# A hand-planned attention and MoE kernel: how a step chooses between two engines, and a second copy of keys made from PSUM

## The chip, the core and the metric

The kernel runs on one core of a Trainium2 chip. The metric is the device time of one execution in microseconds, the median over several runs. The core's engines are TensorE (PE, with its weight loads as PEld), VectorE (DVE), ScalarE (ACT), GpSimd (POOL) and SyncE (SP), which here only issues DMAs.

## The reference

Three layers follow each other on 4 batches of 576 tokens and 512 channels, all in fp32:

```python
# 1. windowed attention, 8 heads of 64: window 32, or 128 with every 4th key for the last 4 heads
scores = where(mask, (q @ k.T) / 8, -1e9); x = softmax(scores) @ v
# 2. mixture of 4 causal attention experts of width 64, the 2 best by x @ w_gate
for e in range(4):
    q, k, v = x @ wq[e], x @ wk[e], x @ wv[e]
    ye = softmax(where(causal, (q @ k.T) / 8, -1e9)) @ v @ wo[e]
    out += gate_weight[e] * ye
# 3. layer norm and MLP 512 -> 2048 -> 512 with a residual
return x + relu(norm(x) @ w_ch1) @ w_ch2
```

## The kernel before

Products that need more than one rounded pass are split: a value is kept as a rounded high part and a low part that holds the rest (h and l in the names), and three matmuls stand for one product.

The work is cut into small generators ("chains"): `turned_qk` and `window` (layer 1, per batch and head pair), `value_tile`, `gate`, `project` and `attend` (layer 2), `out_proj`, then `norm`, `norm_tile`, `decode` and `mlp_group` (layer 3). Each yields its steps one by one, with the engine, a duration in ns that the author assigned, and the times at which its inputs are due. The planner `run_chains` (lines 206 to 250) runs when the program is built: in a loop it looks at the next step of every chain, finds the earliest time at which it could begin on its engine, and issues the step with the lowest score; a tie goes to the chain's rank. The order in which steps are issued is the order of each engine's queue on the chip, and every queue is in order. The times in the planner are only its own; the chip runs each instruction as soon as its queue and its inputs allow.

Most steps name one engine. Steps made with `either` (line 170) name two, and the planner takes the better score: the copies out of PSUM between ACT and DVE (lines 404, 407, 479, 537, 540, 767, 785, 864), the normalisation of a window's scores (line 468) and of an expert's probabilities (line 757) between DVE and POOL, and the shift ahead of the norm's transposes (line 1022) between ACT and DVE. A star at an engine's name says that the step shares an SBUF port with the other of DVE and POOL; in the plan such a step starts only when the other engine's last starred step has ended, 80 ns later. The two choices with POOL are:

```python
t, e = yield either(("DVE*", 370.0), ("POOL*", 620.0), deps=[t])                                # 467
tpp[ee], e = yield either(("DVE*", 70.0 + 0.95 * (n - 64)), ("POOL*", 3.2 * (n - 64)), deps=[t])  # 756
```

where n is 192, 320, 448 or 576 keys for the tiles that have such a step.

`project(b, pr_)` (line 608) computes queries and keys of two experts for one batch, in two halves of 288 tokens each (`hf`); keys come first. Twelve matmuls fill a PSUM bank `pp` whose partitions 0 to 63 belong to one expert and 64 to 127 to the other (line 636). For keys, per expert `ee`: ACT rounds the expert's 64 partitions into `KH` (line 655), a DMA from SP copies these into the other 64 partitions of `KH` (line 657; the planner counts 480 ns of SP and 2200 ns until it lands), and DVE writes what rounding left out into `KL` (line 660, the KL subtract; the tile is called klz in the trace). For queries, ACT rounds into one half of `SQ` (line 648) and DVE writes the rest into the other half (line 650). In `attend` one matmul with 128 rows of `SQ` against both halves of `KH` (line 708) thus gives two of the products, and one against `KL` (line 709) the third. There are 4 batches, 2 expert pairs and 2 halves, so 16 K banks and 32 such casts, transfers and subtracts. The 8 PSUM banks are shared by all chains; `give_bank` gives one back at a planned time.

Of the kernel before, what the change touches and what calls it, by code (L numbers as in the profile page):

```python
# [9 lines left out]
I32 = mybir.dt.int32  # L10
# [13 lines left out]
def windowed_attention_moe_mlp(  # L24
# [15 lines left out]
    nc = tc.nc  # L40
# [10 lines left out]
    HS = S // 2  # L51
# [20 lines left out]
    def bank(name):  # L72

        x = taken.pop(0)
        b = ps1.tile([P, 512], F32, tag=f"bank{x}", name=name)
        lent_banks[id(b)] = x, b
        return b
# [24 lines left out]
    def late(name, dtype):  # L102

        return const.tile([P, 2 * S], dtype, tag="late", name=name, bufs=2)
# [62 lines left out]
    def op(engine, ns, deps=(), tile=None):  # L167
        return "op", ((engine, ns),), deps, tile

    def either(*engines, deps=()):  # L170
        return "op", engines, deps, None

    def acq(tag, n=1):
        return "acq", tag, n

    def key(*k):
        return "key", k
# [4 lines left out]
    def give_bank(b, at):  # L182
        places["bank"].append((at, lent_banks.pop(id(b))[0]))

    def put(*k, at):
        facts[k] = at
# [13 lines left out]
    def resume(c, value):  # L200
        try:
            c[2] = c[1].send(value)
        except StopIteration:
            chains.remove(c)

    def run_chains():
        while chains:
            again = True
            while again:
                again = False  # L210
                for c in sorted(chains, key=lambda c: c[0]):
                    kind = c[2][0]
                    if kind == "acq" and len(places[c[2][1]]) >= c[2][2]:
                        tag, n = c[2][1:]
                        places[tag].sort()
                        at = places[tag][n - 1]
                        if tag == "bank":
                            taken.extend(x for _, x in places[tag][:n])
                            at = at[0]
                        del places[tag][:n]  # L220
                        resume(c, at)
                        again = True
                        break
                    if kind == "key" and c[2][1] in facts:
                        resume(c, facts[c[2][1]])
                        again = True
                        break
            best = None
            for c in chains:
                if c[2][0] != "op":  # L230
                    continue
                _, engines, deps, tile = c[2]
                for name, ns in engines:
                    engine = name.rstrip("*")
                    at = max([free[engine]] + [d + lag[engine] for d in deps])
                    if name != engine:
                        at = max(at, shared["POOL" if engine == "DVE" else "DVE"])
                    change = MODE if engine == "PE" and tile != mode[0] else 0.0
                    score = (at + change + (ns if len(engines) > 1 else 0.0) * 0.5, c[0])
                    if best is None or score < best[0]:  # L240
                        best = score, c, name, ns, at + change, tile
            assert best is not None, [(c[0], c[2]) for c in chains]
            _, c, name, ns, at, tile = best
            engine = name.rstrip("*")
            if name != engine:
                shared[engine] = at + ns + 80.0
            free[engine] = at + ns
            if engine == "PE":
                mode[0] = tile
            resume(c, (at + ns + tail[engine], engine) if len(c[2][1]) > 1 else at + ns + tail[engine])  # L250

    def copy_by(engine, dst, src):
        (nc.scalar.copy if engine == "ACT" else nc.vector.tensor_copy)(dst, src)  # L253
# [54 lines left out]
    def last(k, n):  # L308

        left[k] = left.get(k, n) - 1  # L310
        return left[k] == 0
# [247 lines left out]
    def done_x(b, t):  # L559
        if last(("xh", b), NT + 8):  # L560
            give("xh", t)
# [46 lines left out]
    def project(b, pr_):  # L608
        tx = 0.0
        for c in range(KC):  # L610
            tx = max(tx, (yield key("x", b, c)))
        tw = max((yield key("w", 1)), (yield key("w", 2)))
        tk = (yield key("fr", b - 1, pr_)) if b else 0.0
        tq = yield acq("qk2", 4)
        xh, xl = XH[b], XL[b]

        SQ = [att.tile([P, S], F32R, tag="qk2", name="SQ", bufs=QB) for _ in range(2)]
        KH = [att.tile([P, S], F32R, tag="qk2", name="KH", bufs=QB) for _ in range(2)]
        if b == 0:

            KLZ[pr_] = late(f"klz{pr_}", F32R).rearrange("p (e s) -> p e s", e=2)
            for ee in range(2):
                yield op("POOL", 550.0, [tx])
                nc.gpsimd.memset(KLZ[pr_][64 - 64 * ee:128 - 64 * ee, ee].bitcast(F32), 0.0)
        KL = [KLZ[pr_][:, ee] for ee in range(2)]
        QK[b, pr_] = SQ, KH, KL
        for hf in range(2):
            for wh, wl, isq in ((wkh, wkl, False), (wqh, wql, True)):
                tb = yield acq("bank")
                pp = bank("pp")  # L630
                n = 0
                cs = slice(hf * HS, (hf + 1) * HS)
                for c in range(KC):
                    t = yield op("PE", 400.0, [tb, tx, tw])
                    for ws, xs in ((wh, xh), (wh, xl), (wl, xh)):
                        nc.tensor.matmul(pp[:, :HS], ws[:, c, pr_ * P:(pr_ + 1) * P], xs[:, c, cs],  # L636
                                         start=n == 0, stop=n == 3 * KC - 1)
                        n += 1
                done_x(b, t)
                if b == B - 1 and last("wqk", 8):  # L640
                    put("wqk", at=t)
                ends, dups = [], []
                for ee in range(2):
                    own = slice(64 * ee, 64 * ee + 64)
                    oth = slice(64 - 64 * ee, 128 - 64 * ee)
                    if isq:
                        a = yield op("ACT", 392.0, [t, tq])
                        nc.scalar.mul(SQ[ee][own, cs], pp[own, :HS], SCALE)
                        a = yield op("DVE", 375.0, [a])
                        nc.vector.scalar_tensor_tensor(SQ[ee][oth, cs], pp[own, :HS], SCALE,  # L650
                                                       SQ[ee][own, cs].bitcast(F32),
                                                       op0=ALU.mult, op1=ALU.subtract)
                    else:
                        a = yield op("ACT", 392.0, [t, tq])
                        nc.scalar.copy(KH[ee][own, cs], pp[own, :HS])
                        a2 = yield op("SP", 480.0, [a])
                        nc.sync.dma_start(KH[ee][oth, cs].bitcast(I32), KH[ee][own, cs].bitcast(I32))
                        a2 += 2200.0
                        a = yield op("DVE", 375.0, [a, tk])
                        nc.vector.tensor_tensor(KL[ee][own, cs], pp[own, :HS], KH[ee][own, cs].bitcast(F32),  # L660
                                                op=ALU.subtract)
                        dups.append(a2)
                    ends.append(a)
                give_bank(pp, max(ends))
                put("q", b, pr_, hf, isq, at=max(ends + dups))


    places.update(yh=[0.0], yhs=[0.0], pTh=[0.0] * 2, pT2=[0.0] * 3)
# [453 lines left out]
    with tc.manual_schedule():  # L1122
# [34 lines left out]
        for f in range(NF):  # L1157
            need = min(n for n, (fs, gi) in enumerate(jobs) if f in fs)
            for x in range(2):
                chain(41.0 + f + 0.5 * x if f < 3 else 44.0 + need - 3.0 + 0.5 * x, decode(f, x))  # L1160
        run_chains()


# [26 lines left out]
```

## Time and profile before

| | before |
|---|---|
| median of 3 runs | 770.72 us (770.51 to 774.78) |
| profiled execution | 770.02 us, of which the profile's span is 768.2 us |
| mean granted TensorE clock | 0.982 |
| busy: PE, PEld, DVE, ACT, POOL | 726.0, 603.8, 529.5, 297.0, 192.0 us |
| chain that ended last, by engine | PE 70%, DVE 20%, ACT 4% |

Times in the profile are counted from the span's start. A busy PE isn't PE at its peak, since its matmuls overlap and their ends are modelled. "x <- y" in a list of waits says that x stood idle until y ended; "issue" is a wait for nothing that the profile shows. Names of tiles come without their buffer numbers; s is a bank of scores, pp a bank of projected keys or queries, sc a window's scores, Pp an expert's probabilities, and ppt a bank of transposed ones.

### The profile page before, as it was taken

The page shows a single profiled execution, that of the slowest core. Times are in us where ns is not written, and L with a number is a line of the kernel's source. Part 1 is how long each engine was busy: PE and PEld are TensorE (multiplying, and loading weights), DVE is VectorE, ACT ScalarE, POOL GpSimd, SP SyncE. Part 2 cuts the span into 40 slices and gives each one's busy share as a digit, 9 for nine tenths or more (in the row PEclk, how much of TensorE's full clock was granted, in tenths as well). Part 3 has the DMA queues.
Part 4 walks back from the last instruction along what each step waited for, and adds up shares of the span by engine and source line. Part 5 has one row for each costly group of instructions (what it writes and reads, how often), then busy time and mean ns, then how long its engine had stood idle before and what let it go on. Part 6 is the DMA issues. An engine that isn't in the chain of part 4 may idle for free.

```text
span 768.2 us, 13813 instructions
## 1 busy us (share of the span) xinstructions
PE 726.0 (94%) x5196; PEld 603.8 (79%) x5196; DVE 529.5 (69%) x1342; ACT 297.0 (39%) x793; POOL 192.0 (25%) x233
## 2 busy tenths in 40 slices
PE   6889899999999899799997999999999999999997
PEld 5678778978887789577875888888888888888886
DVE  4756998699778888897467887476474664754333
ACT  3554766466456665774235222122121120211110
POOL 3143231033212213562003434033051140320000
PEclk8979999999999999999999999999999999999999
DMA  8582243223311222210001212011020020100123
GB/s 149 117 166 55 45 93 62 48 59 81 78 32 43 44 64 72 63 56 1 1 0 55 83 56 82 1 56 55 1 83 27 28 83 0 56 1 0 42 82 123
DMA packets 89777, 43.10 MB, mean 56 GB/s; under 512 B 74864, under 2 KB 85104, under 8 KB 89712
## 3 DMA queue, kind: packets, MB, share of 16 engines
q1 hardware_dynamic: 89712, 42.23, 22.2%
q8 instruction: 41, 0.67, 0.4%
q14 instruction: 24, 0.20, 0.1%
HBM read 35.14 MB, written 4.72 MB: 52 GB/s over the span
## 4 chain that ended last, share of the span: by engine, by line
PE 70%; DVE 20%; ACT 4%; issue 2%; SPq 2%; DMA 1%; POOL 1%; DVEq 0%; POOLq 0%; ACTq 0%
PE pout L1102 25%; PE phid L1080 25%; PE pp L636 3%; PE pv L533 3%; PE pwo L853 2%; DVE nm L722 2%; DVE sm L464 2%; DVE mx L457 1%; DVE sc L459 1%; DVE SQ L650 1%; PE po L488 1%; PE ptr L392 1%; PE s L447 1%; PE ppt L475 1%; PE ppt L781 1%
## 5 line engine op out<-in xcount | busy, mean ns | idle before, releaser
L1102 PE MATMUL pout<-wp,ht 128*128 128x512 f32 x864 | 219.7, 395 | 1.5 <-DVE ht L1087 1.3
L1080 PE MATMUL phid<-xn,wp 128*128 128x512 f32 (+1 forms) x960 | 220.0, 373 | 0.5 <-ACT xn L1040 0.5
L1080 PEld LDWEIGHTS phid<-xn,wp 128*128 128x128 f32 x960 | 169.0, 189 | 35.4 <-ACT xn L1040 0.7
L1102 PEld LDWEIGHTS pout<-wp,ht 128*128 128x128 f32 x864 | 160.1, 188 | 37.4 <-DVE ht L1087 2.5
L1111 DVE SCALAR_TENSOR_TENSOR x2a<-pout,rstd,x2a 128x512 f32<-128x512 f32 x124 | 92.2, 748 | 60.9 <-PE pout L1102 59.9
L1085 ACT ACTIVATE ht<-phid 128x512 fp32r<-128x512 f32 (+1 forms) x80 | 44.4, 555 | 203.0 <-PE phid L1080 203.0
L1087 DVE SCALAR_TENSOR_TENSOR ht<-phid,ht 128x512 fp32r<-128x512 f32 (+1 forms) x80 | 50.8, 636 | 65.7 <-ACT ht L1085 65.3
L955 POOL TENSOR_TENSOR d_pw<-d_pw,d_t 128x512 f32<-128x512 f32 x32 | 41.3, 1291 | 180.1 <-DVE d_pw L952 145.0
L468 POOL TENSOR_TENSOR sc<-sc,rs 128x288 f32<-128x288 f32 x35 | 23.3, 672 | 136.0 <-DVE rs L466 117.3
L967 POOL TENSOR_TENSOR wp<-d_pw,wp 128x512 fp32r<-128x512 f32 x32 | 44.4, 1389 | 36.4 <-ACT wp L965 36.4
L757 POOL TENSOR_SCALAR Pp<-Pp,rs 128x512 f32<-128x512 f32 (+3 forms) x34 | 39.3, 1163 | 52.6 <-DVE rs L750 39.8
L939 ACT ACTIVATE d_sq<-ws 128x512 f32<-128x512 f32 x32 | 21.6, 674 | 48.3 <-DVE d_pw L958 23.7
L965 ACT CAST wp<-d_pw 128x512 fp32r<-128x512 f32 x32 | 19.8, 619 | 47.2 <-DVE d_pw L958 41.3
L708 PE MATMUL s<-KH,SQ 128*128 128x64 f32 (+4 forms) x96 | 34.1, 364 | 4.1 <-issue 1.4
L253 ACT COPY pT<-ppt 96x384 f32<-96x384 f32 (+4 forms) x74 | 33.5, 462 | 11.1 <-PE ppt L781 6.3
L724 ACT ACTIVATE Pp<-s,nm 128x192 f32<-128x192 f32 (+3 forms) x64 | 30.4, 475 | 11.7 <-DVE nm L722 8.7
L447 PE MATMUL s<-kT,qT 64*64 64x96 f32 x576 | 34.3, 260 | 0.2 <-ACT kT L253 0.2
L392 PE MATMUL ptr<-ident,nat 72*128 72x72 f32 (+1 forms) x196 | 25.6, 254 | 9.0 <-DMA nat<-in_q_dram 8.2
L475 PE MATMUL ppt<-ident,sc 128*96 128x128 f32 x144 | 26.6, 300 | 7.0 <-POOL sc L468 2.9
L447 PEld LDWEIGHTS s<-kT,qT 64*64 64x64 f32 x576 | 31.9, 147 | 0.6 <-issue 0.5
L781 PE MATMUL ppt<-ident,Pp 128*128 128x128 f32 x160 | 28.8, 282 | 2.8 <-DVE rs L748 1.1
L709 PE MATMUL s<-klz,SQ 128*128 128x64 f32 (+4 forms) x96 | 30.8, 321 | 0.0
(162 smaller groups left out, 1339.8 us busy)
## 6 DMA issues: line engine op xcount, KB each, us to landing
ws<-in_moe_w_ch_dram SPq DMA_DIRECT2D x32, 512.0 KB
nat<-in_q_dram SPq DMA_DIRECT2D x14, 288.0 KB
nat<-in_k_dram SPq DMA_DIRECT2D x14, 288.0 KB
vt<-in_v_dram SPq DMA_DIRECT2D x16, 192.0 KB
out_dram<-x2a SPq DMA_DIRECT2D x12, 256.0 KB
KH<-KH SPq DMA_DIRECT2D x32, 72.0 KB
vt<-in_v_dram SPq DMA_DIRECT2D x32, 48.0 KB
out_dram<-x2b SPq DMA_DIRECT2D x4, 256.0 KB
```

The lines of the kernel that those rows point to most:

```text
L447: nc.tensor.matmul(ps[z, 96 * tt:96 * (tt + 1)], qT[z, 64 * t_:64 * t_ + 64], kT[z, 64 * t_:64 * t_ + 96], start=False, stop=tt == TU - 1)
L475: nc.tensor.transpose(pt[:96, P * tt:P * (tt + 1)], sc[:, tt], ident)
L708: nc.tensor.matmul(ps[:m, :z - a], SQ[ee][:, q0:q0 + m], KH[ee][:, a:z], start=True, stop=False)
L757: (nc.vector if e == "DVE" else nc.gpsimd).tensor_scalar(Ps[ee][:m, 64:n], Ps[ee][:m, 64:n], rs[:m, ee:ee + 1], None, op0=ALU.mult)
L781: nc.tensor.transpose(pt[:, P * (j - 1):P * j], Ps[ee][:, k0:k0 + P], ident)
L955: nc.gpsimd.tensor_tensor(pf, pf, t1.bitcast(F32), op=ALU.add)
L967: nc.gpsimd.tensor_tensor(lo, pf, hi.bitcast(F32), op=ALU.subtract)
L1080: nc.tensor.matmul(ph[:, :n_tok], ws[:, c * P:(c + 1) * P], xs[c], start=n == 0, stop=n == 3 * KC - 1)
L1085: nc.scalar.activation(hh[:, :n_tok], ph[:, :n_tok], AF.Relu)
L1087: nc.vector.scalar_tensor_tensor(hl[:, :n_tok], ph[:, :n_tok], 0.0, hh[:, :n_tok].bitcast(F32), op0=ALU.max, op1=ALU.subtract)
L1102: nc.tensor.matmul(po, a_[:, sl], w_, start=n == 0, stop=n == 3 * len(fs) - 1)
L1111: nc.vector.scalar_tensor_tensor(x2(i), po, rstd[:, i:i + 1], x2(i), op0=ALU.mult, op1=ALU.add)
```

## The change

Two edits. In the planner, the score of a step that may go to either of two engines no longer has half of its duration in it; the time at which it can begin counts alone, as for steps with one engine. In `project`, the second copy of the rounded keys isn't a DMA from SP any more: ACT or DVE, as the planner chooses, copies the expert's partitions of `pp` a second time, into the other 64 partitions of `KH`. This step is issued between the cast and the KL subtract, and the bank goes back when the subtract and the copy have ended.

```diff
@@ run_chains
                     change = MODE if engine == "PE" and tile != mode[0] else 0.0
-                    score = (at + change + (ns if len(engines) > 1 else 0.0) * 0.5, c[0])
+                    score = (at + change + 0.0, c[0])
                     if best is None or score < best[0]:
@@ project
-                ends, dups = [], []
+                ends = []
...
                         a = yield op("ACT", 392.0, [t, tq])
                         nc.scalar.copy(KH[ee][own, cs], pp[own, :HS])
-                        a2 = yield op("SP", 480.0, [a])
-                        nc.sync.dma_start(KH[ee][oth, cs].bitcast(I32), KH[ee][own, cs].bitcast(I32))
-                        a2 += 2200.0
+                        a2, e = yield either(("ACT", 392.0), ("DVE", 380.0), deps=[t, tq])
+                        copy_by(e, KH[ee][oth, cs], pp[own, :HS])
                         a = yield op("DVE", 375.0, [a, tk])
                         nc.vector.tensor_tensor(KL[ee][own, cs], pp[own, :HS], KH[ee][own, cs].bitcast(F32),
                                                 op=ALU.subtract)
-                        dups.append(a2)
+                        a = max(a, a2)
                     ends.append(a)
                 give_bank(pp, max(ends))
-                put("q", b, pr_, hf, isq, at=max(ends + dups))
+                put("q", b, pr_, hf, isq, at=max(ends))
```

## Rows read from the trace of the kernel before

**Rows 1.** Busy us by stage: length, PE, PEld, DVE, ACT, POOL, clock, DMA.

```profile
60.00:80.00 20.00, 18.98 (x188) 17.86 (x187) 13.00 (x45) 10.18 (x31) 3.61 (x4) 1.00 0.23 48
80.00:130.00 50.00, 46.54 (x564) 37.54 (x563) 46.28 (x171) 34.46 (x113) 12.65 (x22) 1.00 0.33 68
130.00:150.00 20.00, 19.50 (x206) 18.41 (x205) 12.17 (x43) 7.46 (x22) 0.72 (x2) 1.00 0.28 63
150.00:200.00 50.00, 47.39 (x537) 39.56 (x535) 46.59 (x167) 33.04 (x113) 17.76 (x25) 1.00 0.28 60
200.00:230.00 30.00, 28.44 (x280) 26.25 (x279) 19.77 (x65) 12.87 (x37) 4.55 (x7) 1.00 0.30 60
230.00:280.00 50.00, 46.01 (x544) 37.70 (x541) 44.32 (x153) 33.07 (x106) 10.61 (x17) 0.97 0.21 48
280.00:300.00 20.00, 19.38 (x157) 18.57 (x151) 15.42 (x42) 10.80 (x29) 5.02 (x4) 1.00 0.28 86
300.00:350.00 50.00, 43.54 (x289) 34.63 (x288) 46.45 (x134) 34.15 (x96) 28.39 (x23) 0.97 0.16 49
400.00:412.00 12.00, 7.45 (x34) 4.64 (x32) 10.12 (x22) 7.83 (x18) 4.04 (x4) 0.94 0.15 45
412.00:768.00 356.00, 351.86 (x1614) 289.17 (x1613) 210.51 (x330) 69.83 (x126) 80.92 (x63) 1.00 0.15 48
```

**Rows 2.** TensorE's waits, whole run: total us, times, longest us.

```profile
PE ppt L475 <- POOL sc L468: 2.9, 6, 1.0
...
PE s L708 <- issue: 1.4, 2, 0.8
...
PE pp L636 <- DVE klz L660: 0.7, 2, 0.6
```

**Rows 3.** TensorE's waits from 0 to 60 us, same columns.

```profile
PE ptr L392 <- DMA nat<-in_q_dram: 8.2, 2, 5.0
```

**Rows 4.** Tile KH: ns min/median/max, first and last start us.

```profile
L655 ACT CAST KH<-pp x32: 377/394/397, 61.6 to 311.6; 64x288 fp32r<-64x288 f32 x32
L657 SPq DMA_DIRECT2D KH<-KH x32: 461/494/1350, 62.0 to 312.0; - x32
```

**Rows 5.** Waits of SP's DMA queue, whole run, same columns.

```profile
SPq L657 <- ACT KH L655: 49.1, 17, 13.6
```

**Rows 6.** Groups by line: count | busy us, mean ns | idle before, releasers.

```profile
L757 POOL TENSOR_SCALAR Pp<-Pp,rs 128x512 f32<-128x512 f32 (+3 forms) x34 | 39.3, 1163 | 52.6 <-DVE rs L750 39.8 <-ACT pT L253 6.6 <-DVE n L731 2.3
...
L757 DVE TENSOR_SCALAR Pp<-Pp,rs 128x128 f32<-128x128 f32 (+3 forms) x30 | 13.0, 455 | 0.0
...
L746 DVE TENSOR_SCALAR sm<-sm 128x2 f32<-128x2 f32 x40 | 8.7, 221 | 1.0 <-ACT Pp L724 0.7
...
L253 DVE COPY kT<-ptr 128x288 f32<-128x288 f32 x16 | 7.3, 456 | 3.8 <-PE ptr L392 3.6
...
L468 DVE TENSOR_TENSOR sc<-sc,rs 128x288 f32<-128x288 f32 x13 | 5.9, 475 | 0.1
```

**Rows 7.** Waits of all engines, columns as in Rows 2.

```profile
ACT KH L655 <- DVE klz L660: 10.0, 12, 1.3
```

**Rows 8.** Chain that ended last, KL subtracts, first and last: start, us.

```profile
68.16 0.46 DVE klz L660
...
303.79 0.47 DVE klz L660
```

**Rows 9.** Busy time by stage, line 655 alone, columns as in Rows 1.

```profile
150.00:200.00 50.00, 0.79 (x2) 1.00 0.28 60
...
300.00:350.00 50.00, 1.55 (x4) 0.97 0.16 49
```

**Rows 10.** Timeline from 334 to 340 us: start us, us, engine, line.

```profile
334.30 0.15 DVE L748 RECIPROCAL rs<-sm 128x2 f32<-128x2 f32 x1
...
335.39 1.04 POOL L963 TENSOR_TENSOR d_pw<-d_pw,g_in 128x512 f32<-128x512 f32 x1 [1.85 <-DVE d_pw L958]
...
335.43 1.03 DVE L746 TENSOR_SCALAR sm<-sm 128x2 f32<-128x2 f32 x1
```


## Prediction

> **What bounds the kernel now.** Read the busy time by stage first [rows 1]. From 412 us to the end, in the second MLP, TensorE works 351.86 of 356 us at a granted clock of 1.00, its 2.4 GHz level. The change adds no instruction there, and of the steps with a choice between engines only a few ahead of the norm's transposes are left, so what it can move lies before 412 us, and it reaches the end by shifting that block. Before it two sorts of stage alternate. In the four projection stages (60 to 80, 130 to 150, 200 to 230, 280 to 300 us) TensorE idles 1.02, 0.50, 1.56 and 0.62 us, 3.7 us of 90, and VectorE is busy 60.4 of 90 us. In the four attention stages (80 to 130, 150 to 200, 230 to 280, 300 to 350 us) VectorE works 44.3 to 46.6 of 50 us, and TensorE idles 3.46, 2.61, 3.99 and 6.46 us, 16.5 us together. There VectorE is as near the bound as TensorE. One more hole stands at 400 to 412 us, 4.55 us, where the last tiles of the attention pass through the norm.
>
> Then read who ended TensorE's waits [rows 2]: behind the first loads (8.2 us in two waits, both before 60 us [rows 3]) they are single waits of 0.3 to 1 us. No one wait explains the 20 us of holes; they are many small misses of an order written out ahead.
>
> **The change part by part, against the profiled execution's 770.0 us (0.7 under the median of the runs, 770.72).**
>
> *The transfer that goes.* 32 DMA issues of 0.494 us leave SP, 15.8 us of its queue [rows 4]. SP waited 49.1 us with such an issue at its head, for the cast that feeds it [rows 5], and loads stood behind it. But TensorE's two waits for loads come before the first such issue, at 62.0 us [rows 3, 4], so I put loads that start earlier at nothing: loading ahead covers them, and without that cover a wait like the 5.0 us one would be the price. What a score matmul waited for the second half of KH is shown nowhere by name: the trace has no landing time for this transfer. The nearest row is the score matmul's own wait with no releaser the profile shows, 1.4 us in two waits [rows 2]. So the gain lies between 0 and 1.4 us, and I take half: **-0.7 us**. In the planner's count the scores also come due about 2.3 us earlier (480 + 2200 ns of transfer against a copy of 380 to 392 ns). This makes work available sooner, but in the projection stages TensorE has other work, as 3.7 us of idle in 90 say.
>
> *The copy that comes.* 32 copies of 64x288 from PSUM. On ScalarE the nearest row is the first copy of the same data, 0.394 us [rows 4]; on VectorE a copy of the same length took 0.456 us [rows 6]; so 0.43 us in the mean and 13.8 us of engine time in all. They don't run beside the work they join. The trace shows ScalarE's second cast waiting 10.0 us in 12 waits for VectorE's subtract of the first half [rows 7], though the two touch different halves of the bank: readers of a bank take turns. Each K bank is therefore held by five or six turns where there were four, 0.86 us longer. The chain that ended last passes through 18 of the 32 subtracts, from 68.16 to 303.79 us [rows 8]. If each of these is pushed by a copy, the cost is 18 x 0.43 = 7.7 us; if TensorE's other work hides all of them it is 0. I choose from two places. TensorE waited twice for a K bank's subtract [rows 2]; 0.86 us more on each is 1.7 us. And 8 of the 32 casts lie in the attention stages, from two in the stage at 150 us to four in that at 300 us [rows 9], where VectorE has no room. ScalarE has 33 to 34 of 50 us there [rows 1], and the rule below takes the engine that is free first, so I charge half of 8 x 0.43, 1.7 us. Together **+3.4 us**; what hides the rest is TensorE's own projection matmuls.
>
> The Trainium skill, page "PSUM — Partial Sum Buffer", section "PSUM bank collisions raise a hardware error", asks that two engines be kept apart per bank and group of 32 partitions, and allows different groups of one bank at once. By that finer form a copy of one half could run beside the other half's subtract, and only 16 of the 32 copies would lengthen a bank's turn: the sum would be 1.7 us lower. The trace bears out the coarser form, a whole bank at a time, and the sum goes by that.
>
> *The choice between two engines.* Before, a step that could go to either engine was ranked by its start plus half its duration. So it stood behind every fixed step that could start within that half, and the slower engine was charged half the difference. Now the start alone counts. Between ScalarE and VectorE durations are close, and little moves. Between VectorE and GpSimd it matters: for line 757 the planner's halves differ by 109 to 541 ns, for line 468 by 125 ns. On VectorE stand 30 steps of line 757 (13.0 us busy) and 13 of line 468 (5.9 us) [rows 6]. I estimate that a third of both moves, 14 steps, which takes 6.3 us off VectorE. Nothing before shows how many would move: the bounds are 0 and all of them, 18.9 us. A stage can't give back more than TensorE's holes in it, 16.5 us in all; with TensorE busy over 90% there, I count half of the relief: **-3.2 us**.
>
> Against it stand two costs. A step of line 757 takes 1163 ns on GpSimd and 455 on VectorE [rows 6], so its data comes some 0.7 us later. TensorE's waits for GpSimd were 2.9 us [rows 2] for the 35 steps of line 468 that ran there (48 windows less the 13 on VectorE), 0.083 us each; 14 more at that price are **+1.2 us** (bounds 0, and 14 x 0.7 = 9.9 us if all are waited for). And GpSimd stops VectorE: at 335.43 us a step on 128x2 values took 1.03 us while a GpSimd step of 1.04 us ran, where a step of that size took 0.15 us just before [rows 10]. The mean of that line is 221 ns [rows 6], so over 40 of them about 40 x 0.07 = 2.8 us was lost beside 34 steps of line 757 on GpSimd; ten more cost **+0.8 us** (bounds 0, and 10 x 0.9 = 9 us if each meets such a step). Page "SBUF — State Buffer" of the Trainium skill, section "Who interferes with whom", says that the second of two such instructions fully blocks until the first ends; the row agrees, and this speaks against the change.
>
> The sum: 770.0 - 0.7 + 3.4 - 3.2 + 1.2 + 0.8 = **771.5 us**. Beyond it, every later step may land in another place. One such miss is worth at most what the largest hole costs today, 4.55 us, in either direction; from this comes the forecast's own range, 766 to 777.
>
> **The rivals.** *VectorE is relieved for good (faster).* If the copies go mostly to ScalarE and two thirds of the steps leave VectorE, the holes of the four attention stages close by 60%: 16.5 x 0.6 = 9.9 us, 760 us. For it: VectorE at 93% in these stages. Against it: TensorE is itself at 92 to 95% in three of them.
>
> *The K banks' turns become the bound (slower).* Each copy stands between a cast and a subtract, and a copy on VectorE waits at the head of its queue for the cast, with the reductions and subtracts of other tiles behind it. This decides once 20 copies shift the chain (20 x 0.43 = 8.6 us); with 25 of 32 it is 770.0 + 10.8 = 781 us. For it: 18 subtracts on the chain. Against it: 0.7 us of waits for these banks now.
>
> *GpSimd's long steps come on the path (slower).* The two halves of a tile both go to GpSimd, since VectorE's turn is counted from GpSimd's end. If 13 of them are waited for in full, 13 x 0.7 = 9 us, 779 us. For it: the 1.03 us row. Against it: 0.083 us a step now.
>
> *The change doesn't do what it says.* The score matmuls did not wait for the transfer, the copies hide, and hardly a step moves: 770 us.
>
> **How the numbers follow.** About 1%, from 763.0 to 778.4 us, can't be told from no change. The forecast 0.52 (0.03 of it beyond each bound), no effect 0.08, VectorE relieved 0.17 (0.15 below 763.0), K banks 0.14 (0.11 above 778.4), GpSimd 0.09 (0.05 above). So faster 0.18, slower 0.19, within 1% 0.63. Under 760 us I leave out 0.09 (half of the faster case), over 782 us 0.09 (part of both slower cases): the range is 760 to 782.
>
> **What would show it.** Right: TensorE's idle in the projection stages stays near 4 us, the nameless waits of the score matmul are gone, line 757 on GpSimd rises from 34 to some 44, VectorE's busy time in the attention stages falls though 32 copies were added. Wrong: TensorE's waits for a K subtract rise above 3 us (banks), waits for lines 757 or 468 on GpSimd above 6 us (GpSimd), idle in the attention stages under 8 us (relief), or the hole at 400 us shut or doubled, which no term here counts. Most exposed is the third of the steps that I let move: it is an estimate from the planner's lines, not a row.

## The result and the profile after

The changed kernel takes 761.91 us (median of 4 runs, 759.07 to 762.34), the kernel before in the same comparison 770.62 us (770.04 to 774.78). The medians differ by 8.7 us, or 1.1%; the ratio, which goes by all runs, is 0.9868, with an interval from 0.9826 to 0.991, so 1.3% faster. The profiled execution took 761.55 us, of which 759.8 us are its span. In the listings of after, and of every kernel below that has after's `project`, the line numbers from 657 on are one lower: line 757 of before is L756, the KL subtract of line 660 is L659.

The busy time of the engines over the span, from the page of after:

```profile
PE 722.1 (95%) x5196; PEld 603.9 (79%) x5196; DVE 542.4 (71%) x1397; ACT 293.6 (39%) x792; POOL 163.2 (21%) x211
```

VectorE is busy 12.9 us more than before (529.5), GpSimd 28.8 us less (192.0). TensorE's idle time, span less busy, went from 42.2 to 37.7 us, its busy time from 726.0 to 722.1: 4.5 and 3.9 us, the 8.4 us between the two spans.

The busy time by stage of after, the stages and columns of [rows 1] (length, PE, PEld, DVE, ACT, POOL, clock, DMA share, GB/s):

```profile
60.00:80.00 20.00, 19.08 (x202) 18.09 (x200) 11.75 (x38) 9.40 (x28) 7.90 (x12) 1.00 0.18 33
80.00:130.00 50.00, 45.01 (x533) 38.83 (x534) 47.28 (x171) 33.97 (x115) 11.54 (x23) 1.00 0.38 80
130.00:150.00 20.00, 17.91 (x187) 15.48 (x186) 12.76 (x43) 8.44 (x25) 0.10 (x1) 1.00 0.03 5
150.00:200.00 50.00, 47.33 (x547) 41.27 (x547) 46.20 (x158) 31.51 (x107) 8.11 (x18) 1.00 0.33 71
200.00:230.00 30.00, 30.00 (x316) 26.90 (x315) 24.65 (x90) 16.29 (x48) 2.93 (x6) 1.00 0.13 29
230.00:280.00 50.00, 47.51 (x539) 41.36 (x538) 44.84 (x159) 33.52 (x105) 7.97 (x13) 1.00 0.20 48
280.00:300.00 20.00, 17.96 (x149) 15.14 (x148) 19.12 (x61) 13.22 (x37) 3.37 (x3) 1.00 0.09 27
300.00:350.00 50.00, 46.30 (x339) 37.69 (x339) 47.99 (x155) 35.10 (x99) 14.32 (x11) 1.00 0.13 43
400.00:412.00 12.00, 12.00 (x58) 9.94 (x57) 6.75 (x10) 2.17 (x4) 0.00 (x0) 1.00 0.01 1
```

Three things are to be seen against [rows 1], whose stretches are kept here. After's own stages lie a little elsewhere (its first K matmul starts at 65.4 us, that of before at 59.7), so sums of stretches say more than a single one. The hole at 400 to 412 us (4.55 us) is gone. TensorE's idle in the four attention stages fell from 16.5 to 13.85 us, that in the four projection stages rose from 3.7 to 5.05. And the granted clock, which was 0.97 at 230 to 280 and at 300 to 350 us and 0.94 at 400 to 412 us, is 1.00 in all of them. In before it fell behind idle time of TensorE, here from 310 us on:

```profile
310.00:315.00 5.00, 2.11 (x16) 1.91 (x15) 4.46 (x15) 4.10 (x12) 4.24 (x3) 0.99 0.13 30
315.00:318.30 3.30, 3.30 (x18) 2.46 (x17) 2.11 (x9) 1.33 (x4) 2.04 (x3) 0.50 0.02 5
```

Of the first 5 us TensorE was busy 2.11; in the next 3.3 us it was busy throughout, at half the clock, the 1.2 GHz level. So this hole was paid for twice, once as idle time and once in clock.

The first MLP matmul of line 1080 starts at 302.1 us where it started at 323.1, the last transpose of line 1031 at 388.4 us where it was 416.0. These marks overstate the lead: the number of matmuls is the same, and what runs earlier here is missing later. From that transpose to the end of the span after takes 371.4 us, before 352.2, and 8.4 us of the 27.6 reach the end of the span (8.7 by the medians of the runs).

TensorE's waits in after (us in total, times, longest us), those that answer [rows 2]; then VectorE's wait for ScalarE's cast, which is new, and the groups by line that answer [rows 6]:

```profile
PE ppt L475 <- POOL sc L468: 4.5, 5, 2.3
...
PE ppt L780 <- DVE klz L659: 1.7, 1, 1.7
PE pp L636 <- DVE klz L659: 1.6, 2, 1.4
```

```profile
DVE KH L253 <- ACT KH L655: 8.5, 11, 2.0
```

```profile
L756 DVE TENSOR_SCALAR Pp<-Pp,rs 128x256 f32<-128x256 f32 (+3 forms) x58 | 22.0, 418 | 0.0
...
L253 DVE CAST KH<-pp 64x288 fp32r<-64x288 f32 x18 | 8.2, 455 | 8.7 <-ACT KH L655 8.5
...
L756 POOL TENSOR_SCALAR Pp<-Pp,rs 128x128 f32<-128x128 f32 (+2 forms) x6 | 6.7, 1124 | 24.6 <-DVE rs L749 17.7 <-ACT V L549 6.9
...
L253 ACT CAST KH<-pp 64x288 fp32r<-64x288 f32 x14 | 5.5, 394 | 0.2
...
L468 DVE TENSOR_TENSOR sc<-sc,rs 128x288 f32<-128x288 f32 x7 | 3.7, 534 | 0.1
```

Of the 64 steps of line 757, 58 run on VectorE (30 before) and 6 on GpSimd (34 before): the opposite of what was forecast. Line 468 went the other way, 13 to 7 on VectorE. The copies split 18 to VectorE and 14 to ScalarE, 13.7 us of engine time, and those on VectorE stood 8.5 us at the head of its queue until ScalarE's cast of the same bank had ended.

### The profile page after: what moved, and what is told of

Read it like the earlier page. It is cut to its first block, busy times and chain, and to the rows that moved or that the text cites. A ratio compares the mean times of both kernels' runs of the same rounds, so it can differ in the third digit from the quotient of the medians.

```text
span 759.8 us, 13731 instructions
## 1 busy us (share of the span) xinstructions
PE 722.1 (95%) x5196; PEld 603.9 (79%) x5196; DVE 542.4 (71%) x1397; ACT 293.6 (39%) x792; POOL 163.2 (21%) x211
## 4 chain that ended last, share of the span: by engine, by line
PE 78%; DVE 16%; ACT 2%; issue 1%; DMA 1%; SPq 1%; POOL 0%; DVEq 0%; POOLq 0%; ACTq 0%
PE pout L1101 26%; PE phid L1079 26%; PE pp L636 4%; PE s L447 3%; PE pwo L852 3%; PE ppt L780 2%; PE ppt L475 2%; PE pv L533 2%; PE ptr L392 2%; PE po L488 2%; PE py L801 1%; PE s L707 1%; DVE Pp L756 1%; DVE xl L509 1%; DVE klz L659 1%
## 5 line engine op out<-in xcount | busy, mean ns | idle before, releaser
L954 POOL TENSOR_TENSOR d_pw<-d_pw,d_t 128x512 f32<-128x512 f32 x32 | 41.5, 1296 | 217.0 <-DVE d_pw L951 186.9
L468 POOL TENSOR_TENSOR sc<-sc,rs 128x288 f32<-128x288 f32 x41 | 27.2, 668 | 144.2 <-DVE rs L466 135.1
L253 ACT COPY pT<-ppt 96x384 f32<-96x384 f32 (+4 forms) x66 | 30.3, 466 | 20.5 <-PE ppt L475 13.3
L723 ACT ACTIVATE Pp<-s,nm 128x320 f32<-128x320 f32 (+3 forms) x64 | 30.4, 476 | 12.6 <-DVE nm L721 11.4
L707 PE MATMUL s<-KH,SQ 128*128 128x64 f32 (+4 forms) x96 | 32.5, 346 | 2.2 <-ACT pTh L253 0.9
L780 PE MATMUL ppt<-ident,Pp 128*128 128x128 f32 x160 | 28.8, 282 | 4.0 <-DVE klz L659 1.7
L462 ACT ACTIVATE sc<-sc 128x288 f32<-128x288 f32 x48 | 21.0, 445 | 26.0 <-DVE sc L459 25.8
L1110 DVE SCALAR_TENSOR_TENSOR x2b<-pout,rstd,x2b 128x512 f32<-128x512 f32 x32 | 24.0, 749 | 9.3 <-PE pout L1101 9.1
## 6 DMA issues: line engine op xcount, KB each, us to landing
vt<-in_v_dram SPq DMA_DIRECT2D x16, 192.0 KB, 3.6
```

The lines of the kernel that those rows point to most:

```text
L707: nc.tensor.matmul(ps[:m, :z - a], SQ[ee][:, q0:q0 + m], KH[ee][:, a:z], start=True, stop=False)
L780: nc.tensor.transpose(pt[:, P * (j - 1):P * j], Ps[ee][:, k0:k0 + P], ident)
L954: nc.gpsimd.tensor_tensor(pf, pf, t1.bitcast(F32), op=ALU.add)
L1110: nc.vector.scalar_tensor_tensor(x2(i), po, rstd[:, i:i + 1], x2(i), op0=ALU.mult, op1=ALU.add)
```

## The experiments

The theory at the start: the gain comes from the 28 steps of line 757 that left GpSimd for VectorE, and the copies cost little. Its rivals: the gain is the order in which steps are issued, whichever engine they go to; and the result is an accident of one order. Each kernel below is timed against the kernel before, whose median in the five comparisons was 770.24 to 771.71 us. "Rule" stands for the new choice between two engines, "order" for the whole sequence of issues that the planner writes.

### The two edits alone

The rule alone has, of the change, only the score; the transfer stays as in before. The copy alone has after's `project` with the old score.

```diff
-  score = (at + change + (ns if len(engines) > 1 else 0.0) * 0.5, c[0])
+  score = (at + change + 0.0, c[0])            # rule alone: this, in before
```

> The rule of choice alone, with the transfer from SP left as before; in its program 49 of the 64 steps of line 757 stand on VectorE (30 before, 58 after the change). Theory A (the gain of 8.7 us comes from line 757 going to VectorE, which takes 0.42 us there against 1.16 us on GpSimd): 762 to 765 us. Theory B (the gain comes from the transfer that is gone): 770 to 772 us. Theory C (it is only another order, and any order differs by some us): anything from 760 to 778 us, with no relation to the count of line 757.

> The copy alone, with half of the duration still in the score; in its program 25 steps of line 757 stand on VectorE and 39 on GpSimd. Theory A: 770 to 774 us (the copies cost engine time, and nothing else is won). Theory B: 761 to 764 us. Theory C: anything from 760 to 778 us.

Measured: rule alone 755.1 us, ratio 0.9774 [0.9747, 0.9802], 49 of line 757's steps on VectorE. Copy alone 776.3 us, 1.0049 [1.0027, 1.007], 25 on VectorE. The two edits pull in opposite directions, and the change is the smaller for its copies: the rule gives 16.6 us against this comparison's 771.71, the copy costs 4.6.

### How much one order differs from another

Each kernel issues its steps in one order, so a difference of two kernels holds the luck of two orders. To size that, a constant of the planner was moved by 2 ns, which leaves the instructions the same but for the engine of some two-engine steps and reorders them.

```diff
-    MODE = 141.0
+    MODE = 139.0                               # second order
```

```diff
-    tail = {... "DVE": 95.0, "POOL": 70.0 ...}
+    tail = {... "DVE": 97.0, "POOL": 70.0 ...}  # third order
```

> The kernel before with one of the planner's constants, the price of changing the matmul tiling, at 139 in place of 141 ns: no instruction is another, but nearly all queues are in another order (line 757: 31 on VectorE, 33 on GpSimd). Theories A and B: within 3 us of before, 768 to 774 us. Theory C: off by 5 us or more.

> The changed kernel with the same constant at 139 ns: another order, and 56 steps of line 757 on VectorE. Theories A and B: within 3 us of the changed kernel, 759 to 765 us. Theory C: off by 5 us or more, so that it may come out at 768 us as well.

> The kernel before with the planner's tail of a VectorE step at 97 in place of 95 ns: the same instructions in another order (27 steps of line 757 on VectorE). Theory C, which the first four runs favour (two reorderings moved by +6 and +15 us): 765 to 785 us, 5 us or more off in most such orders. Theory A: 768 to 775 us.

> The changed kernel with the tail of a VectorE step at 97 ns: another order, 57 steps of line 757 on VectorE. Theory C: between 755 and 780 us. Theory A: 759 to 766 us, and under the kernel before whatever the order.

> The new rule of choice with the transfer from SP, and the tail of a VectorE step at 97 in place of 95 ns: a second order of that kind (53 steps of line 757 on VectorE). Theory D, formed from the first eight runs: the rule is worth some 15 to 20 us whatever the order, and the copies cost 13 us of it again. Then 748 to 762 us. Theory C (the order alone): anything from 755 to 780 us.

> The new rule of choice with the transfer from SP, and the price of changing the tiling at 139 ns: a third order of that kind, with only 39 steps of line 757 on VectorE. Theory D: 748 to 764 us. Theory C: anything from 755 to 780 us. If it is line 757's engine that counts, this one is the slowest of the three by 3 us or more.

> The copies with the old rule of choice, and the planner's tail of a VectorE step at 97 in place of 95 ns: a second order of that kind (the first took 776.3 us; three orders of the old rule with the transfer took 770.6 to 777.6 us). If the copies cost under the old rule what they cost under the new one (10 us over three orders each, 13.4 us in one and the same order): 778 to 790 us. If the old rule hides them: 770 to 777 us.

Measured, in us (interval of the ratio in brackets; the first column is the order of the change itself):

| | as it is | MODE 139 | DVE tail 97 | mean |
|---|---|---|---|---|
| old rule, transfer (before) | 770.6 | 777.58 [1.003, 1.0097] | 773.15 [0.9996, 1.0044] | 773.8 |
| old rule, copies | 776.3 [1.0027, 1.007] | not run | 784.93 [1.0152, 1.0202] | 780.6 (of two) |
| new rule, transfer | 755.1 [0.9747, 0.9802] | 755.64 [0.976, 0.9858] | 758.6 [0.98, 0.9883] | 756.4 |
| new rule, copies (after) | 761.9 [0.9826, 0.991] | 776.64 [1.0041, 1.0085] | 761.58 [0.9807, 0.9908] | 766.7 |

The rule is no accident: with the transfer kept, all three orders of it lie 12 us or more below all three orders of the old rule, 17.4 us in the mean; with the copies it is 13.9 us by the means, and 18.9 over the two orders that both rows have. The copies cost 10.3 us under the new rule in the mean of three orders (6.8, 21.0 and 3.0), and 8.7 under the old one in the mean of two (5.7 and 11.8); the means of the table differ by 6.8 there, because one of them holds an order that was not run with copies. What is partly an accident is the size for the whole change: before against after is 8.7, 0.9 and 11.6 us in the three orders. At 0.9 us, with MODE 139, nothing of the rule's gain is left beside the copies.

The number of line 757's steps on VectorE doesn't go with the time: 49, 39 and 53 in the three orders of the rule with the transfer, which lie within 3.5 us, and 56 in the MODE 139 order of after, 14.7 us slower than after with 58. That speaks against the theory.

### The engine of line 757 by itself

```diff
-  tpp[ee], e = yield either(("DVE*", 70.0 + 0.95 * (n - 64)), ("POOL*", 3.2 * (n - 64)), deps=[t])
+  tpp[ee], e = (yield op("DVE*", 70.0 + 0.95 * (n - 64), [t])), "DVE"       # in before: all on VectorE
```

```diff
+  e = ("DVE", "POOL")[ee]                                                   # in after: half and half
+  tpp[ee] = yield op(("DVE*", "POOL*")[ee], (70.0 + 0.95 * (n - 64), 3.2 * (n - 64))[ee], [t])
```

> The kernel before with all 64 steps of line 757 given to VectorE; the old score and the transfer stay. If the rule's gain comes from keeping this line off GpSimd: 755 to 764 us. If it comes from when a step with a choice gets its turn: 768 to 776 us.

> The changed kernel with line 757 split by hand, the first half of a tile on VectorE and the second on GpSimd (32 and 32, as the kernel before has 30 and 34); the new score and the copies stay. If the rule's gain comes from keeping this line off GpSimd: 770 to 780 us. If not: 758 to 768 us.

Measured: with the old rule and all 64 on VectorE 780.87 us, 1.0124 [1.0073, 1.0174], slower than before. With the new rule and 32 on GpSimd 765.34 us, 0.9911 [0.9877, 0.9946], 3.4 us slower than after and still faster than before. The theory falls: moving the steps to VectorE by hand doesn't bring the gain, and moving 26 of them back doesn't undo it. Each of the two is one order, and the interval of the second overlaps that of after; but neither went where the theory puts it (755 to 764 us and 770 to 780 us).

### The engine or the turn

The one score of before does two things. It picks the engine of a step, and it ranks the step against the next steps of all other chains, its turn. These two kernels, with the transfer kept, take the new score for one and the old one for the other.

```diff
+  late = at + change + (ns if len(engines) > 1 else 0.0) * 0.5
+  picks.append((late, at + change, name, ns))
   ...
+  late, at, name, ns = min(picks, key=lambda x: x[0])   # turn only: engine by the old score,
+  score = (at, c[0])                                    #            turn by the start
   ...
+  late, at, name, ns = min(picks, key=lambda x: x[1])   # engine only: engine by the start,
+  score = (late, c[0])                                  #              turn by the old score
```

> The kernel before with the rule of choice taken apart: which engine a step takes still goes by its start plus half its duration, but its turn among all steps goes by its start alone. The transfer stays. If the gain of the rule (17.5 us over three orders each) lies in the turn: 753 to 762 us. If it lies in the choice of the engine: 768 to 778 us.

> The other part: the engine goes by the earliest start alone, the turn by start plus half the duration as before. The transfer stays. If the gain lies in the turn: 768 to 778 us. If it lies in the choice of the engine: 753 to 762 us.

> The turn alone by the earliest start, and the planner's tail of a VectorE step at 97 in place of 95 ns: a second order of that kind, so that the order's own spread is seen. Turn: 753 to 764 us. Engine: 768 to 778 us.

> The engine alone by the earliest start, and the tail of a VectorE step at 97 ns: a second order of that kind. Turn: 768 to 780 us. Engine: 753 to 764 us.

Measured (second value: the same with the DVE tail at 97): turn only 761.2 us, 0.9874 [0.9841, 0.9907], and 755.3, 0.9814 [0.9791, 0.9837]; engine only 766.68, 0.9959 [0.9938, 0.9979], and 776.22, 1.0077 [1.0058, 1.0097]. In the mean the turn alone gives 758.3 us, where both halves together gave 756.9 in the same two orders; the engine alone gives 771.5, where the old rule gave 771.9. Order by order the turn alone gives 9.4 and 17.9 us, the engine alone 3.9 us and then 3.1 us of loss. So the gain is that of the turn. All steps with a choice got the new turn at once, the copies out of PSUM too; which of them bring the gain was not separated. The turn also explains the count: engine only has 25 and 15 steps of line 757 on VectorE (30 and 27 by the old rule), which is the direction that the prediction forecast; turn only has 55 and 53.

What the turn does is seen ahead of the second MLP. The stretches from 60 to 280 us and from 280 to 420 us (columns as above) of before, then of turn only, turn only with tail 97, engine only, and engine only with tail 97:

```profile
60.00:280.00 220.00, 206.86 (x2302) 177.33 (x2301) 182.13 (x640) 131.08 (x418) 49.90 (x76) 0.99 0.27 58
280.00:420.00 140.00, 128.04 (x804) 104.22 (x799) 103.96 (x264) 72.22 (x187) 44.19 (x35) 0.98 0.12 38
```

```profile
60.00:280.00 220.00, 211.20 (x2295) 184.95 (x2294) 191.94 (x670) 123.74 (x405) 27.70 (x57) 0.97 0.30 60
280.00:420.00 140.00, 132.20 (x846) 106.69 (x844) 118.48 (x315) 65.86 (x177) 32.16 (x24) 1.00 0.12 38
```

```profile
60.00:280.00 220.00, 211.58 (x2356) 185.10 (x2356) 193.58 (x687) 130.63 (x424) 32.96 (x63) 1.00 0.30 64
280.00:420.00 140.00, 133.02 (x814) 105.80 (x813) 115.35 (x285) 64.66 (x169) 33.47 (x26) 1.00 0.10 34
```

```profile
60.00:280.00 220.00, 205.84 (x2288) 178.80 (x2287) 175.62 (x621) 132.97 (x429) 55.25 (x80) 0.98 0.27 59
280.00:420.00 140.00, 129.53 (x813) 105.03 (x812) 104.96 (x262) 72.84 (x190) 44.27 (x35) 0.95 0.11 34
```

```profile
60.00:280.00 220.00, 204.77 (x2285) 178.18 (x2285) 174.45 (x617) 131.97 (x430) 66.41 (x93) 0.99 0.26 57
280.00:420.00 140.00, 125.32 (x788) 102.70 (x787) 100.96 (x252) 68.35 (x181) 46.72 (x38) 0.94 0.13 39
```

From 60 to 280 us VectorE is busy 9.8 and 11.5 us more with the new turn than in before. Of this 5.9 and 4.4 us are steps of lines 757 and 468, which now stand on VectorE; 3.9 and 7.1 us are other work. TensorE is busy 4.3 and 4.7 us more. In the first order that is no more work, for it ran 2295 matmuls where before ran 2302, at a granted clock of 0.97 against 0.99; in the second it ran 54 more. With the new engine choice alone both are busy less than in before, VectorE mostly because fewer steps of these two lines stand on it. The kernel with the old rule and line 757 all on VectorE did not fill it: VectorE is busy 178.28 us there, 18.2 of them with line 757 (10.9 in before). After itself has TensorE at 206.84 us there, as its projections begin 5.7 us later than before's; its lead shows from 280 to 420 us, 133.63 against 128.04.

Over both stretches the two turns part clearly, among the kernels that keep the transfer. With the new turn (the rule alone in three orders, the turn alone in two) TensorE idles 13.1 to 17.5 us from 60 to 420 us and runs 3139 to 3194 matmuls there, at a clock of 0.98 to 1.00. With the old turn (before in three orders, the engine alone in two, line 757 all on VectorE) it idles 24.6 to 31.6 us and runs 3057 to 3100, at 0.97 to 0.99. The least and the most idle kernel of the new turn (the rule alone, and with tail 97), then of the old (engine only, and line 757 all on VectorE):

```profile
60.00:420.00 360.00, 346.94 (x3194) 295.07 (x3193) 307.25 (x959) 197.07 (x598) 88.15 (x108) 1.00 0.24 54
```

```profile
60.00:420.00 360.00, 342.53 (x3187) 292.19 (x3186) 302.94 (x958) 197.34 (x603) 75.03 (x98) 1.00 0.23 52
```

```profile
60.00:420.00 360.00, 335.37 (x3099) 283.83 (x3098) 280.57 (x882) 205.81 (x619) 99.52 (x115) 0.97 0.21 49
```

```profile
60.00:420.00 360.00, 328.39 (x3057) 278.37 (x3055) 285.29 (x913) 200.20 (x604) 51.58 (x76) 0.97 0.21 49
```

In the mean of each group the idle time differs by 12.7 us and the time of the kernel by 17.0; what makes up the rest, the clock for one, was not separated.

This agrees with one reading of the code: a step whose turn carries half its duration is issued behind fixed steps that start later than it could, and since queues are in order, what stands behind it in its chain is late as well. That TensorE's holes shrink with the turn is shown; that it is by this mechanism and no other is argued from the code.

### What the copies cost in one and the same order

This kernel lets the planner count after's copy and issues the DMA of before in its place, with the planned times unchanged; TensorE's and GpSimd's queues are the same as after's. The next issues each copy twice, under the plan of one. The last puts all 32 copies on ScalarE, under the same plan.

```diff
   a2, e = yield either(("ACT", 392.0), ("DVE", 380.0), deps=[t, tq])
-  copy_by(e, KH[ee][oth, cs], pp[own, :HS])
+  nc.sync.dma_start(KH[ee][oth, cs].bitcast(I32), KH[ee][own, cs].bitcast(I32))   # transfer
+  copy_by(e, ...); copy_by(e, ...)                                                # twice
+  copy_by("ACT", KH[ee][oth, cs], pp[own, :HS])                                   # on ScalarE
```

> The changed kernel with the planner untouched (it still counts a copy, on ScalarE or VectorE), but in place of each of the 32 copies the transfer from SP is issued. TensorE's and GpSimd's queues are the same, instruction by instruction; VectorE and ScalarE lack the copies. If the transfer's latency was what the scores waited for (theory B): slower than the changed kernel by 2 us or more, 764 to 772 us, with new waits of the score matmul. If the copy is worth nothing or costs (the sum's +3.4 us against -0.7): equal or faster, 756 to 762 us.

> The changed kernel with each of the 32 copies made twice in a row, the planner untouched: 13.8 us more of engine time, in the same order. If a copy costs what the sum counted (3.4 us for 32): 764 to 767 us. If copies lie beside TensorE's other work: 761 to 763 us. If the K banks' turns bound the stage (18 or more of them on the chain): 769 us or more.

> The changed kernel, the planner untouched, but all 32 copies run on ScalarE (18 of them stood on VectorE): VectorE is rid of 8.2 us of copies and of 8.5 us in which its queue waited at a copy for ScalarE's cast. If the 13.4 us that the copies cost are VectorE's queue: 750 to 756 us. If they are the longer turns at a K bank, whichever engine copies: 759 to 764 us.

Measured: transfer 748.5 us, 0.97 [0.9666, 0.9734]; copies 761.9; copies on ScalarE 756.33, 0.9814 [0.9783, 0.9845]; each copy twice 777.05, 1.0055 [1.0033, 1.0076]. So the copies cost 13.4 us over a transfer in the same order, and a second set of them 15.1, each for 13.7 us of engine time. A part of the second price is clock: from 60 to 331 us it was 0.97 with each copy twice and 1.00 with one set. The transfer in after's plan is the fastest kernel of the study and beats before and after, by 22.1 and 13.4 us. That its order is better than those of the rule alone (755.1 to 758.6 us) is one order against three; why is not known.

Where in the run it goes is seen from the first and last matmul of the K banks (the tile's list: ns min/median/max of the 64, first and last start), with the transfer, with copies, on ScalarE, and twice:

```profile
L636 PE MATMUL pp<-xh,wkh x64: 290/296/383, 62.1 to 302.6; 128*128 128x288 f32 x64
```

```profile
L636 PE MATMUL pp<-xh,wkh x64: 290/297/383, 65.4 to 314.6; 128*128 128x288 f32 x64
```

```profile
L636 PE MATMUL pp<-xh,wkh x64: 290/297/382, 64.6 to 309.6; 128*128 128x288 f32 x64
```

```profile
L636 PE MATMUL pp<-xh,wkh x64: 288/297/384, 65.8 to 331.1; 128*128 128x288 f32 x64
```

From first to last K matmul it is 240.5 us with the transfer, 249.2 with copies and 245.0 with copies on ScalarE; with each copy twice it is 265.3 (65.8 to 331.1). So of the 13.3 us between the first two spans (746.5 and 759.8), 8.7 lie in the stretch where the K banks are made, and 1.3 behind it. The other 3.3 lie ahead of the first K matmul, where no copy has run. They go with the granted clock, 0.99 at 50 to 60 us with the transfer and 0.67 with the copies, under the same queue of TensorE and behind the same wait of it for line 468 (2.09 and 2.04 us); why the clock fell behind one of them only is open, so these 3.3 us aren't shown to be the copies'. Without them the price is 10.0 us, near the 10.3 of the mean over orders. The other runs bear out that clock is not all of it: after's run at the highest mean clock, 0.993, took 759.07 us, those with the transfer 746.82 to 749.77 at 0.988 to 0.991.

On ScalarE the copies cost 5.6 us less by the medians and 4.2 by the ratios to before, whose intervals overlap; from the first to the last K matmul it is 4.2 us. The wait at the head of VectorE's queue is gone, and one at the subtract takes its place, VectorE's wait (us, times, longest) in that kernel:

```profile
DVE klz L659 <- ACT KH L253: 11.1, 11, 2.4
```

VectorE waits about as long here (11.1 us) as in after (8.5 us for the casts, and 2.2 in its subtracts for ScalarE's copies), but is rid of the 8.2 us of the 18 copies. That VectorE's time is what the copies take is therefore shown for some 4 us of their price. How the rest divides between longer turns of the K banks and ScalarE's time was not separated.

## Why the prediction was wrong

It forecast 771.5 us and no change that can be measured; 761.9 us came, inside the range and on the faster side of the 1% bound. That it lies inside the range is luck: the rule's three terms came to -1.2 us and it gave -17.4 in the mean of its orders, copy and missing transfer came to +2.7 and cost 10.3, two errors that stand against each other. Step by step:

- **The choice rule (-3.2, +1.2, +0.8)** failed in its sign of movement and by far in its size. "A third of both moves" from VectorE to GpSimd: line 757 moved 28 steps the other way; only line 468 lost 6. The step that failed is earlier: the prediction read the score as a charge on the slower engine and priced that. It said in the same sentence that a step "stood behind every fixed step that could start within that half", and gave this no term. That half of the edit is worth the whole gain, and the other half, the one priced, is worth nothing that shows (771.5 against 771.9 us).
- **"A stage can't give back more than TensorE's holes in it, 16.5 us in all."** That bound was drawn too narrow: it left out the hole at 400 us, which shut, and the clock behind holes. The rule's three orders with the transfer lie 15 to 19 us under the mean of the old ones.
- **GpSimd blocks VectorE (+0.8)** had the sign wrong, since fewer GpSimd steps came, and its price per step of line 757 doesn't hold. The mean of the 128x2 step fell from 221 ns [rows 6] to 175 ns with 6 steps of line 757 on GpSimd in place of 34. But it was 172 ns with 32 of them there (half and half) and 168 with none (all on VectorE). The three kernels' lines, in this order:

```profile
L745 DVE TENSOR_SCALAR sm<-sm 128x2 f32<-128x2 f32 x40 | 7.0, 175 | 1.1 <-ACT Pp L723 0.8
```

```profile
L745 DVE TENSOR_SCALAR sm<-sm 128x2 f32<-128x2 f32 x40 | 6.9, 172 | 1.3 <-ACT Pp L723 1.1
```

```profile
L746 DVE TENSOR_SCALAR sm<-sm 128x2 f32<-128x2 f32 x40 | 6.7, 168 | 1.0 <-ACT Pp L724 0.7
```

  A single step does wait, as [rows 10] shows; how many do so differs from order to order and not with the number of these steps. The Trainium skill, page "SBUF — State Buffer", section "Who interferes with whom", has a VectorE instruction in a mode that takes the shared ports and a GpSimd instruction exclude each other, so that the second waits for the first to end; [rows 10] agrees, with 1.03 us beside a GpSimd step of 1.04 us.
- **GpSimd steps late (+1.2).** TensorE's waits for line 468 on GpSimd rose from 2.9 to 4.5 us, in one wait fewer; +1.6 from other steps than the ones named.
- **The copy (+3.4)** had the direction right and its size wrong: 8.7 and 10.3 us in the means over orders, 3.0 to 21.0 in single ones, 13.4 in one and the same order, 10.0 of it from the first K matmul on. The sentence that fell is "what hides the rest is TensorE's own projection matmuls". The bound of 7.7 us, by 18 subtracts on the chain, is passed too: it counted the bank's turns alone, and left out VectorE's own time, some 4 us of which came back when ScalarE made all copies. The rival with the K banks gave 10.8 us for 25 of 32 copies, and was nearer. Its sign in the trace, TensorE's waits for a K subtract above 3 us, came narrowly: 1.6 us at line 636 and 1.7 at a transpose, where before has 0.7 and 0.3. The larger part of the cost stands in no wait for these subtracts.
- **The finer rule for banks**, by which the copies would cost 1.7 us less, went the wrong way as well. The runs don't show what the hardware would allow there: the waits between cast, copy and subtract end at semaphores of the program, so "readers of a bank take turns" is shown of this program alone.
- **The transfer (-0.7)** lay within its bounds of 0 and 1.4 us, at the end that gives nothing: with the transfer put back in after's plan the nameless wait of the score matmul doesn't return, so that wait was not shown to be the transfer's, though SP stood 41.5 us with such an issue at its head (49.1 before [rows 5]). The transfers landed 2.0 us after their issue there, which the trace of before doesn't show.
- **"Every later step may land in another place", ±4.55 us.** Mis-sized: 2 ns in one constant moved before by 7.0 us (5.9 against the runs of before beside it) and after by 14.7.

Of the signs named in advance for right, two came: the projection stages' idle stayed near 4 us (5.05), and the nameless waits went. The rise of line 757 on GpSimd and a fall of VectorE's busy time did not. Of those for wrong two came, the hole at 400 us that shut and the waits for K subtracts. Faster came, but not by the rival named for it: VectorE was not relieved, it was busier. (Its 93% in that rival is 92% by [rows 1].)

## What to carry to other kernels

When a planner's score does two things, such as choosing an engine and giving a turn, price each by itself, and try each by itself; here all of a gain of 13.6 to 17.4 us was in the one that looked like a side effect. When an order is written out by a program, compare edits over several orders made by moving a constant a little, before crediting an edit with less than the spread; and keep two opposed edits apart, since the best kernel had only one of these. Here 32 copies on VectorE and ScalarE cost 10 us or more for 13.7 us of engine time, while a transfer that is issued early, and that nobody waits for, cost nothing that the runs show.

## What the runs showed that was not expected

- The spread over orders is not small: 770.6 to 777.6 us for before, 761.6 to 776.6 for after, with intervals of ±0.2 to ±0.5%. In the MODE 139 order of before, the hole ahead of the norm's transposes is the largest wait of TensorE, 14.0 us where before (second line) has 4.4:

```profile
PE pxt L1031 <- ACT xg L1024: 14.0, 7, 3.2
```

```profile
PE pxt L1031 <- ACT xg L1024: 4.4, 4, 2.0
```

- The engine with the shorter duration needn't be the faster placing: under the old turn all of line 757 on VectorE, at 448 ns a step, took 780.9 us, and 34 of its steps on GpSimd, at 1163 ns, 771.5.
- The granted clock at 50 to 60 us differed from 0.67 to 0.99 between kernels whose TensorE queue was the same up to there, and the first K matmul came 3.3 us later with the lower one. Executions of one kernel differ too: after with the DVE tail at 97 took 755.67 us at a mean clock of 0.995, and 761.44, 761.72 and 763.48 at 0.988, 0.986 and 0.982. No run tells why.
- Five results lay outside every range that was expected for them: the rule alone (755.1 us, under all), line 757 all on VectorE (780.87, above both), the transfer in after's plan (748.5, under both), the engine alone in its first order (766.68, between the two), and the copies on ScalarE (756.33, between the two).
